# Fetching a weight matrix in pairs of parts with 4 KB rows, and one seam transfer per half

## The chip, the core and the metric

The kernel runs on one core of a Trainium2 chip. Five engines work side by side, each through its own instructions in order: TensorE (PE in the profile; its weight loads are PEld), VectorE (DVE), ScalarE (ACT), GpSimd (POOL) and SyncE (SP), which here only issues DMA transfers. ScalarE and GpSimd issue a few transfers too. The metric is the time of one execution on the device in microseconds; a lower time is better.

## The reference

A gated linear recurrence over complex decays, and then a two-layer network with ELU on its output:

```python
mag = np.sqrt(a_re * a_re + a_im * a_im)
scale = np.minimum(mag, 0.999) / (mag + 1e-06)
a_re_n, a_im_n = (a_re * scale, a_im * scale)
for t in range(S):                       # S = 768, for B = 4, H = 8, D = 48
    ar, ai = (a_re_n[:, :, t, :, None], a_im_n[:, :, t, :, None])
    new_re = ar * S_re - ai * S_im
    new_im = ar * S_im + ai * S_re
    kv = np.einsum('bhd,bhe->bhde', k[:, :, t], v[:, :, t])
    S_re, S_im = (new_re + kv, new_im)
    y[:, :, t] = np.einsum('bhd,bhde->bhe', q[:, :, t], S_re)
x = y.transpose(0, 2, 1, 3).reshape(B * S, H * D)          # 3072 x 384
h = x @ w_in                                               # w_in: 384 x 2048
g = np.where(h > 0.0, h, np.exp(np.minimum(h, 0.0)) - 1.0)
out = g @ w_out                                            # w_out: 2048 x 384
```

The two weight matrices arrive as 64-bit floats, everything else as 32-bit floats.

## The kernel before

**Steps.** The work is cut into twelve steps u = 0 to 11. A step takes 128 positions of two sequences: it loads a (re and im), q, k and v, turns a into running decays (logarithms, sums by matmul, exponentials, sines), scales and rotates q and k by them (`gated`), transposes both on TensorE, multiplies scores and states (`scores`, `states`, `values`), and passes its result through the network (`inner` is the first matmul, `elu` the activation, `project` the second matmul). Steps 0 and 1 and the loading of the weights make up the start; from step 3 on the network's matmuls are done with fewer products, from sums of the weights that are made in between.

**Order.** Every engine works through one order of named pieces. For the start it is written out by hand, in the list `first`; the rest comes from a table of places (`plan`). `warm` pieces are matmuls without a use, put where TensorE would be idle.

**Weights.** `w_in` is held as [128, 3, 2048]: partition p, block i of the contraction, column. Heads are 48 rows wide and a half is 64 partitions, so rows 0 to 47 of a half come from a head of its own and the last 16 from a third of another head. Eight parts of 256 columns are fetched by `fetch("in", m)`, each in four transfers (two of 48 partitions, two of 16), as raw 32-bit words, two to a number, with 2 KB to a row. Their raw words lie in tiles under the tags `g0` and `g1` (parts 0 to 3) and `w64` (parts 4 to 7). `w_out` ([128, 16, 384]) follows in eight parts of its own through `w64`. `rounded` makes a part's 32-bit floats on VectorE with four operations; `convert` steps through them at the places that the list gives: two with one source (L671, L674), a sum of both (L677) and the last that writes `w_in` or `w_out` (L679). These places do not move.

**Seam.** After a step's `values`, its result stands as x (three blocks) and y (the fourth group of heads). `seam` moves the rows of y into the gaps of 16 partitions of x, one small transfer for each half j and block i, six in all. At u = 0 and u = 1 the transfers are spread over SyncE, ScalarE and GpSimd; later they are on GpSimd, with three of one step on SyncE.

## Time and profile before

| | |
|---|---|
| median of 3 runs | 620.69 us (619.47 to 622.34) |
| the profiled execution | 621.27 us, its span 619.5 us |
| TensorE busy | 605.0 us (98%), 6980 matmuls |
| VectorE busy | 503.0 us (81%), 781 operations |
| ScalarE busy | 415.8 us (67%) |
| GpSimd busy | 176.5 us (28%) |
| DMA | 65.54 MB, mean 106 GB/s |
| granted TensorE clock | 0.997 |

The span runs from the first to the last instruction of the profiled execution, and all times inside it count from its start. A row of the timeline gives start, duration, engine, source line, operation, what it writes and reads, and in brackets the idle time of the engine before it with what ended it. A line that begins with `SPq`, `ACTq` or `POOL ... DMA_DIRECT2D` is the issue of a transfer, not the transfer.

### The profile page before, as it was taken

What the parts mean: (1) busy time and instruction counts of PE and PEld (TensorE: products, weight loads), DVE (VectorE), ACT (ScalarE), POOL (GpSimd) and SP (SyncE); (2) the same over time, 40 slices, a digit from 0 to 9 for tenths busy, and PEclk for the clock granted to TensorE, in tenths of its full rate; (3) what the DMA queues carried; (4) which work ended last, traced back from release to release, by engine and by line L of the source; (5) the groups of instructions that cost most, each with busy time, mean ns of one, the idle gap of its engine ahead of it and who ended that gap; (6) DMA issues with size and microseconds to landing.
All of it is one profiled execution on the core that took longest, in us unless ns stands there. A gap on an engine that the chain in (4) does not pass through costs nothing. (4 is left out here: it accounts for less than half of the span.)

```text
span 619.5 us, 16960 instructions
## 1 busy us (share of the span) xinstructions
PE 605.0 (98%) x6980; PEld 550.0 (89%) x6980; DVE 503.0 (81%) x781; ACT 415.8 (67%) x681; POOL 176.5 (28%) x240
## 2 busy tenths in 40 slices
PE   8799999999999999999999999999999999999996
PEld 6678887567899999999999999999999999999996
DVE  5788878667599899888898898899898888984482
ACT  5975674675787667776777876777777777661350
POOL 2000100103113534523524434534534422422000
PEclk9989999999999999999999999999999999999999
DMA  9978739630653253746556545546673647342101
GB/s 165 183 139 136 152 111 239 145 65 22 91 90 58 53 97 81 143 95 123 118 104 123 118 103 121 125 99 122 126 134 85 142 80 132 73 87 66 53 2 32
DMA packets 192179, 65.54 MB, mean 106 GB/s; under 512 B 168116, under 2 KB 181596, under 8 KB 192092
## 3 DMA queue, kind: packets, MB, share of 16 engines
q1 hardware_dynamic: 187920, 62.72, 51.6%
q0 software_dynamic: 3520, 1.20, 1.7%
q8 instruction: 57, 0.93, 0.7%
q10 hardware_dynamic: 652, 0.44, 0.3%
q14 instruction: 30, 0.25, 0.2%
HBM read 48.91 MB, written 4.80 MB: 87 GB/s over the span
## 5 line engine op out<-in xcount | busy, mean ns | idle before, releaser
L1410 PE MATMUL mlp<-w_out,g 128*128 128x192 f32 x640 | 112.1, 328 | 0.0
L1410 PEld LDWEIGHTS mlp<-w_out,g 128*128 128x128 f32 x640 | 104.3, 190 | 3.3 <-DVE ee L1424 0.6
L1132 POOL TENSOR_TENSOR S<-S,T 128x384 f32<-128x384 f32 x36 | 38.0, 1057 | 150.0 <-DVE S L1130 83.1
L1388 DVE TENSOR_TENSOR g<-g 128x512 f32<-128x512 f32 x80 | 60.7, 774 | 6.3 <-PE mlp L1410 4.7
L1301 PE MATMUL mlp<-x,w_in 128*128 128x256 f32 x288 | 64.1, 381 | 0.0
L1301 PEld LDWEIGHTS mlp<-x,w_in 128*128 128x128 f32 x288 | 54.7, 192 | 8.5 <-issue 0.6
L1569 ACT ACTIVATE ee<-g 128x512 f32<-128x512 f32 x63 | 39.6, 629 | 29.5 <-DVE g L1564 26.8
L1548 PE MATMUL mlp<-x,w_in 128*128 128x128 f32 x424 | 56.3, 276 | 0.1
L1410 PE MATMUL mlp<-w,g 128*128 128x192 f32 x320 | 54.5, 329 | 0.0
L1410 PEld LDWEIGHTS mlp<-w,g 128*128 128x128 f32 x320 | 51.8, 190 | 0.6
L1548 PEld LDWEIGHTS mlp<-x,w_in 128*128 128x128 f32 x424 | 51.7, 192 | 0.6 <-DVE g L1564 0.3
L1281 POOL DMA_DIRECT2D x<-y x62 | 30.6, 499 | 72.2 <-ACT y L1177 40.4
L1570 ACT ACTIVATE ee<-ee 128x512 f32<-128x512 f32 x72 | 45.4, 631 | 2.3
L1573 DVE SCALAR_TENSOR_TENSOR g<-ee,g 128x512 f32<-128x512 f32 x63 | 42.4, 682 | 2.3 <-ACT ee L1570 2.3
L1561 ACT COPY g<-mlp 128x512 f32<-128x512 f32 x36 | 20.9, 584 | 29.4 <-PE mlp L1548 29.4
L1564 DVE TENSOR_TENSOR g<-g,mlp 128x512 f32<-128x512 f32 x45 | 30.8, 684 | 8.9 <-PE mlp L1548 4.1
L1291 ACT ACT_TABLE_LOAD x24 | 30.8, 1283 | 2.1 <-issue 1.6
L921 ACT ACTIVATE n<-w 64x384 f32<-64x384 f32 (+1 forms) x60 | 28.1, 486 | 5.2 <-PE w L906 4.4
L1548 PE MATMUL mlp<-x,g 128*128 128x128 f32 x224 | 30.1, 277 | 0.0
L1268 ACT COPY x<-y 128x384 f32<-128x384 f32 x20 | 8.6, 482 | 30.9 <-PE y L1160 30.9
L1075 POOL COPY qt<-kt 32x512 f32<-32x512 f32 x24 | 24.4, 1017 | 16.3 <-PE mlp L1548 10.2
L1548 PE MATMUL y<-x,w_in 128*128 128x128 f32 x216 | 28.5, 275 | 0.0
(218 smaller groups left out, 1369.7 us busy)
## 6 DMA issues: line engine op xcount, KB each, us to landing
w<-in_moe_w_out_dram SPq DMA_DIRECT2D x8, 768.0 KB, 4.7
g<-in_moe_w_in_dram SPq DMA_DIRECT2D x24, 256.0 KB, 3.1
g<-in_moe_w_out_dram SPq DMA_DIRECT2D x24, 256.0 KB, 3.0
w<-in_moe_w_in_dram SPq DMA_DIRECT2D x16, 288.0 KB, 5.8
vn<-in_v_dram SPq DMA_DIRECT2D x24, 192.0 KB, 5.6
qt<-kt SPq DMA_DIRECT2D x72, 64.0 KB, 2.0
kt<-cs SPq DMA_DIRECT2D x72, 64.0 KB, 2.3
q<-in_q_dram SPq DMA_DIRECT2D x11, 384.0 KB, 4.7
```

Source lines behind the costliest of these rows:

```text
L921: nc.scalar.activation(out=flat(x[key][to, n : n + 1]), in_=t[of], func=AF.Exp, scale=sign)
L1132: eng.tensor_tensor(out=new_s, in0=new_s, in1=wide, op=ALU.mult)
L1281: eng.dma_start(out=x["x"][ds(j * HP + D, G), i], in_=x["y"][ds(j * HP + i * G, G)])
L1291: nc.scalar.preload_act_table_set(name)
L1301: nc.tensor.matmul(t[:, e], lhsT=w_in[:, i, ts(f + e, C)], rhs=x["x"][:, i], start=(i == 0), stop=(i == NI - 1),)
L1388: nc.vector.tensor_tensor(out=S_of(u, k, h), in0=a, in1=b, op=op)
L1410: nc.tensor.matmul(to, lhsT=a[:, m], rhs=b[:, m], start=(first and h == 0 and m == 0), stop=False, skip_group_check=True,)
L1548: nc.tensor.matmul(x["c" + c][:, ts(m, C)], lhsT=a[:, m], rhs=x["mix"][p], start=(p == BANKS[c][0] and m == 0), stop=False, skip_group_che ...
L1564: nc.vector.tensor_tensor(out=part(u, to), in0=part(u, a), in1=part(u, b), op=op)
L1569: nc.scalar.activation(out=e, in_=part(u, of), func=AF.Relu, scale=-1.0)
L1570: nc.scalar.activation(out=e, in_=e, func=AF.Exp, scale=-1.0)
L1573: nc.vector.scalar_tensor_tensor(out=part(u, to), in0=nat[u]["e", to], scalar=-1.0, in1=part(u, of), op0=ALU.add, op1=ALU.max,)
```

## The change

**What it does.** w_in is fetched in four pairs of parts, 512 columns at a time, so that a row is 4 KB; the raw words lie in one half or the other of `w_out`, which is not filled yet then. `rounded` still makes one part of 256 columns at a time, from three rows of 256 numbers inside the pair's words. In the list `first`, four `fetch` entries stand where eight stood: the first pair at the place of the first part, the second pair behind the loads of a(1) and v(0) and ahead of q and k of step 1, the third at the place of the old fifth part, and the last at the place of the old seventh. A seam has one transfer for each half (16 x 3 x 256), on SyncE for the first half of steps 0 and 1, on ScalarE for their second half, and on GpSimd after that, but for one half of one step.

```diff
         if kind == "in":
             n = WF * DM // NI
-            dst, cols = w_in[:, :, ts(m, n)], ts(m, 2 * n)
-            tag = "g" + str(m // 2) if m < 4 else "w64"
-            t = sb.tile([C, WF * DM, 2], U32, tag=tag, bufs=2, name="w64")
-            words = t.rearrange("p (i n) two -> p i (n two)", i=NI)
+            dst, cols = None, ts(m, 4 * n)
+            t = w_out[:, ts(m % 2, NF // 2)].rearrange("p f n -> p (f n)").bitcast(U32)
+            words = t.rearrange("p (i n) -> p i n", i=NI)
...
-                last = moe_w_in[ds((2 * NI + j) * D, D), cols].rearrange("(i d) n -> d i n", i=NI)
+                last = moe_w_in[ds((2 * NI + j) * D, D), cols].rearrange("(d i) n -> d i n", i=NI)
...
     def rounded(kind, m):
-        w, dst = raw.pop((kind, m))
-        lo, hi = w[:, :, 0], w[:, :, 1]
         f = sb.tile([C, WF * DM], U32, tag="wt", bufs=2, name="wf")
         r = sb.tile([C, WF * DM], U32, tag="wt", bufs=2, name="wr")
+        if kind == "in":
+            n = WF * DM // NI
+            dst, w = w_in[:, :, ts(m, n)], raw[kind, m // 2][0]
+            w = w.rearrange("p (i n two) -> p i n two", i=NI, two=2)[:, :, ts(m % 2, n)]
+            f, r = (x.rearrange("p (i n) -> p i n", i=NI) for x in (f, r))
+        else:
+            w, dst = raw.pop((kind, m))
+            w = w.rearrange("p (f n) two -> p f n two", f=WF)
+            f, r = (x.rearrange("p (f n) -> p f n", f=WF) for x in (f, r))
+        lo, hi = w[:, :, :, 0], w[:, :, :, 1]
...
     def seam(u):
         x = nat[u]
         for j in range(2):
-            for i in range(NI):
-                eng = nc.scalar if u < 2 and j else nc.gpsimd
-                if u == 0 and i == NI - 1 or u == PAIRED and j:
-                    eng = nc.sync
-                eng.dma_start(
-                    out=x["x"][ds(j * HP + D, G), i], in_=x["y"][ds(j * HP + i * G, G)]
-                )
+            eng = nc.sync if u < 2 and not j or u == PAIRED and j else nc.gpsimd
+            if u < 2 and j:
+                eng = nc.scalar
+            eng.dma_start(out=x["x"][ds(j * HP + D, G)], in_=x["y"][ds(j * HP, D)])
```

In the list `first`, `(fetch, "in", 1)` to `(fetch, "in", 7)` are taken out at their places, and `(fetch, "in", 1)`, `2` and `3`, now pairs, stand in again, for example:

```diff
-        (load_a, 1), (fetch, "in", 1), (load_v, 0), (angles, 0, 0), (fetch, "in", 2),
+        (load_a, 1),  (load_v, 0), (angles, 0, 0), (fetch, "in", 1),
```

**Where the instructions stand.** TensorE's order is the same before and after. Three places of the others follow. First SyncE's transfers at the start, before (`w` with a number is a raw tile of w_in's words, or for `a`, `q` and `k` of step 1 a shared tile; the sizes are those of the first side):

```order
L662 DMA w_146<-in_moe_w_in_dram 48x3x512 x2
L662 DMA w_146<-in_moe_w_in_dram 16x3x512 x2
L611 DMA q<-in_q_dram 128x16x48
L611 DMA k<-in_k_dram 128x16x48
L611 DMA w_193<-in_a_re_dram 128x16x48
L611 DMA w_193<-in_a_im_dram 128x16x48
L662 DMA w_196<-in_moe_w_in_dram 48x3x512 x2
L662 DMA w_196<-in_moe_w_in_dram 16x3x512 x2
L607 DMA vn_72<-in_v_dram 128x8x48 x2
L662 DMA w_205<-in_moe_w_in_dram 48x3x512 x2
L662 DMA w_205<-in_moe_w_in_dram 16x3x512 x2
L611 DMA w_328<-in_q_dram 128x16x48
```

and after:

```order
L661 DMA w_out<-in_moe_w_in_dram 48x3x1024 x2
L661 DMA w_out<-in_moe_w_in_dram 16x3x1024 x2
L611 DMA q<-in_q_dram 128x16x48
L611 DMA k<-in_k_dram 128x16x48
L611 DMA w_192<-in_a_re_dram 128x16x48
L611 DMA w_192<-in_a_im_dram 128x16x48
L607 DMA vn_72<-in_v_dram 128x8x48 x2
L661 DMA w_out<-in_moe_w_in_dram 48x3x1024 x2
L661 DMA w_out<-in_moe_w_in_dram 16x3x1024 x2
L611 DMA w_321<-in_q_dram 128x16x48
```

Twice the bytes of w_in stand ahead of q, k and a, none between a and v, and twice the bytes again ahead of q and k of step 1 (which had two parts ahead of them in two places).

Second, SyncE from the first seam (x<-y) on, before:

```order
L1281 DMA x<-y 16x256 x2
L607 DMA vn_73<-in_v_dram 128x8x48 x2
L662 DMA w_605<-in_moe_w_in_dram 48x3x512 x2
L662 DMA w_605<-in_moe_w_in_dram 16x3x512 x2
L611 DMA ar<-in_a_re_dram 128x16x48
L611 DMA ai<-in_a_im_dram 128x16x48
L662 DMA w_614<-in_moe_w_in_dram 48x3x512 x2
L662 DMA w_614<-in_moe_w_in_dram 16x3x512 x2
L662 DMA w_808<-in_moe_w_in_dram 48x3x512 x2
L662 DMA w_808<-in_moe_w_in_dram 16x3x512 x2
```

and after:

```order
L1286 DMA x<-y 16x3x256
L607 DMA vn_73<-in_v_dram 128x8x48 x2
L661 DMA w_out<-in_moe_w_in_dram 48x3x1024 x2
L661 DMA w_out<-in_moe_w_in_dram 16x3x1024 x2
L611 DMA ar<-in_a_re_dram 128x16x48
L611 DMA ai<-in_a_im_dram 128x16x48
L661 DMA w_out<-in_moe_w_in_dram 48x3x1024 x2
L661 DMA w_out<-in_moe_w_in_dram 16x3x1024 x2
L1286 DMA x<-y 16x3x256
L661 DMA w_914<-in_moe_w_out_dram 128x2x768
```

The second seam's first half has come onto SyncE, behind the last pair and ahead of the first part of w_out.

Third, VectorE around the first conversion (`wr` and `wf` are its two working tiles; L860 is the first step of the angles' turns, n their tile), before:

```order
L671 TENSOR_SCALAR wr<-w_146 128x768
L674 TENSOR_SCALAR wf<-w_146 128x768
L677 ISA wf<-wf,wr 128x1536
L860 SCALAR_TENSOR_TENSOR n<-n,w 128x384
L866 TENSOR_SCALAR cs<-n 128x8x48
```

and after:

```order
L678 TENSOR_SCALAR wr<-w_out 128x768
L681 TENSOR_SCALAR wf<-w_out 128x768
L684 ISA wf<-wf,wr 128x1536
L866 SCALAR_TENSOR_TENSOR n<-n,w 128x384
L872 TENSOR_SCALAR cs<-n 128x8x48
```

Nothing moved here; the operations on a part now read from `w_out`, and their line numbers are six to seven higher.

More of the change, by code (lines that the diff above doesn't have):

```diff
@@ L677, in rounded @@
         yield nc.vector.tensor_tensor(out=f, in0=f, in1=r, op=ALU.add)
-        n = dst.shape[-1]
         nc.vector.scalar_tensor_tensor(
-            out=dst.bitcast(U32), in0=hi.rearrange("p (b n) -> p b n", n=n), scalar=TOP,
-            in1=f.rearrange("p (b n) -> p b n", n=n), op0=ALU.bitwise_and, op1=ALU.bitwise_or,
+            out=dst.bitcast(U32), in0=hi, scalar=TOP, in1=f, op0=ALU.bitwise_and,
+            op1=ALU.bitwise_or,
         )
@@ L1759 @@
         (states, 0, 1), (angles, 1), *2 * [(warm, 2)], (scaled, 1), (noted, 0), (values, 0, 1),
-        (carry_on, 0), (fetch, "in", 3), (convert,), (ends, 1), (convert,), (seam, 0),
-        (load_v, 1), (table, "trig_and_small", 1), (convert,), (warm, 1), (turns, 1), (convert,), (waves, 1), (inner, 0, 2), (inner, 0, 0), (fetch, "in", 4), (load_a, 2), (fetch, "in", 5),
+        (carry_on, 0),  (convert,), (ends, 1), (convert,), (seam, 0),
+        (load_v, 1), (table, "trig_and_small", 1), (convert,), (warm, 1), (turns, 1), (convert,), (waves, 1), (inner, 0, 2), (inner, 0, 0), (fetch, "in", 2), (load_a, 2),
         (table, "natural_log_exp_and_others", 1), (gated, 1, 0), (convert,), (gated, 1, 1),
@@ L1765 @@
         (inner, 0, 4), *2 * [(convert,)], (transposed, 1, "k", 1), (convert,), (warm, 4),
-        (scores, 1, 1), (values, 1, 0), (fetch, "in", 6), (convert,), (fetch, "in", 7),
+        (scores, 1, 1), (values, 1, 0), (fetch, "in", 3), (convert,),
         (states, 1, 1), (convert,), (elu, 0, 0), (convert,), (elu, 0, 4), (values, 1, 1),
```

## The prediction

> **What bounds the kernel now.** I read the busy time by stretch first. Its columns are busy microseconds (with instruction counts) of TensorE, its weight load, VectorE, ScalarE and GpSimd, then the granted clock, the share of the DMA engines and GB/s.
>
> ```profile
> 0.00:42.00 42.00, 35.20 (x409) 29.16 (x410) 30.97 (x46) 33.52 (x62) 5.44 (x33) 1.00 1.03 161
> 42.00:614.00 572.00, 569.64 (x6572) 520.79 (x6572) 471.67 (x735) 382.24 (x620) 171.04 (x207) 1.00 0.51 102
> 42.00:45.00 3.00, 3.00 (x7) 1.79 (x8) 2.09 (x4) 1.85 (x2) 0.00 (x0) 0.50 0.69 130
> ```
>
> From 42 us on TensorE is busy 569.6 of 572 us: an order of matmuls that the change leaves as it is, and that nothing outside TensorE can shorten. So the question is when the matmul row at 42.38 us starts, plus what the half clock in the third row costs just there. Next, the timeline ahead of that point, in order of time: VectorE, then TensorE, then VectorE again.
>
> ```profile
> 16.89 0.56 DVE L860 SCALAR_TENSOR_TENSOR n<-n,w 128x384 f32<-128x384 f32 x1 [3.12 <-ACT n L859]
> 20.00 0.55 DVE L1003 TENSOR_TENSOR k<-k,n 128x384 f32<-128x384 f32 x1
> 24.02 0.96 DVE L1020 TENSOR_TENSOR qg<-q,cs 128x768 f32<-128x768 f32 x1
> 25.25 1.12 PE L1034 MATMUL w<-ident,qg 128*96 128x128 f32 x8
> 26.30 1.15 PE L1082 MATMUL w<-qt,kt 96*64 96x64 f32 x32
> 27.38 1.99 PE L1115 MATMUL mlp<-vn,kg 64*128 64x48 f32 x32
> 29.40 0.56 DVE L1128 TENSOR_TENSOR S<-mlp,T 128x384 f32<-128x384 f32 x1 [1.14 <-PE mlp L1115]
> 38.96 0.95 DVE L999 TENSOR_TENSOR w<-w,n 128x768 f32<-128x768 f32 x1
> 40.70 0.56 DVE L671 TENSOR_SCALAR wr<-w 128x768 uint32<-128x768 uint32 x1
> 41.25 0.18 DVE L968 COPY once<-w 48x32 f32<-48x32 f32 x1
> 41.58 0.38 PE L970 MATMUL w<-once,pair 48*128 48x32 f32 x2 [0.37 <-DVE once L968]
> 42.38 2.77 PE L854 MATMUL w<-n,sum_turns 128*128 128x384 f32 x4
> 44.95 5.59 PE L1301 MATMUL mlp<-x,w_in 128*128 128x256 f32 x24
> ```
>
> The chain is tight. L1020 ends at 24.98 and the transposes that read qg start at 25.25; these end at 26.37, with the scores (L1082) already starting; L1115 follows, and VectorE waited for it before L1128. From there VectorE runs without a gap to L968, which TensorE waits for. The only wide gap is the 3.12 us ahead of L860. A delay that is larger than that gap leaves therefore arrives at 42.38 us nearly whole.
>
> The third view is the DMA side: the stretches (same columns as above), k of the first step as SyncE issues it and the time from its issue to its landing, and VectorE's first conversion.
>
> ```profile
> 2.00:10.00 8.00, 8.00 (x34) 6.89 (x33) 5.30 (x4) 2.67 (x6) 2.33 (x17) 1.00 1.09 193
> 10.00:38.00 28.00, 23.27 (x291) 18.62 (x289) 22.26 (x38) 27.36 (x48) 0.65 (x1) 1.00 1.22 184
> 71.00:73.00 2.00, 2.00 (x11) 1.77 (x10) 1.97 (x4) 1.97 (x4) 0.00 (x0) 1.00 1.08 211
> 76.00:78.00 2.00, 2.00 (x11) 1.77 (x10) 1.85 (x4) 0.94 (x2) 0.00 (x0) 1.00 0.88 356
> 38.00:40.00 2.00, 2.00 (x61) 1.81 (x61) 1.97 (x4) 1.86 (x6) 0.00 (x0) 1.00 0.10 26
> 6.50 4.88 SPq L611 DMA_DIRECT2D k<-in_k_dram  x1
> DMA to landing us min/median/max: 9.3/9.3/9.3
> 11.76 0.56 DVE L671 TENSOR_SCALAR wr<-w 128x768 uint32<-128x768 uint32 x1
> ```
>
> From 2 to 38 us the queue never rests, at 193 and then 184 GB/s: whatever is put ahead delays all that is behind it. k landed at 6.50 + 9.3 = 15.8 us. VectorE converts the first part of w_in at 11.76 with no wait, so that part had landed by then.
>
> **The change, part by part.**
>
> *A longer first fetch.* What stands ahead of q and k grows from one part, 2 x 288 + 2 x 96 = 768 KB, to two: 0.786 MB more, or 4.2 us at the 188 GB/s that I put between the rows of 184 and 211. All four transfers must land before the first conversion. Counted in bytes, a and the part (1.573 MB) are through at 2 + 8.2 = 10.2 us, k (another 0.786) at 14.4; k landed 1.4 later, so the part landed near 11.6, at 11.76 at the latest. With 4.2 us more that is 15.8 to 16.0; I take 16.0, since the last transfers, of 16 partitions, come slowly (the row 38:40, where little else is left).
>
> Whether rows of 4 KB move faster no row says. The two ends are the w_in stretch at 71 us (2 KB rows, transfers of 48 and 16 partitions, 211 GB/s) and the w_out stretch at 76 us (3 KB rows, 128 partitions, 356). I take the w_in end, since the new transfers keep 48 and 16 partitions and the strided source, and differ from it in row length alone. [...]
>
> *Conversion.* The two one-source operations now read three rows of 256 words at a pitch of 1024, where they read one run of 768, and still write one run.
>
> ```profile
> L671 DVE TENSOR_SCALAR wr<-w 128x768 uint32<-128x768 uint32 x12 | 6.7, 558 | 1.1 <-DMA w<-in_moe_w_in_dram 1.1
> L674 DVE TENSOR_SCALAR wf<-w 128x768 uint32<-128x768 uint32 x12 | 6.7, 556 | 0.0
> L679 DVE SCALAR_TENSOR_TENSOR w_in<-w,wf 128x768 uint32<-128x768 uint32 x8 | 7.6, 952 | 0.0
> ```
>
> [...] The bounds are 0.557 (unchanged) and 0.952 each. [...] Price: 0.395 us each, 16 of them, 6.3 us of VectorE, of which only three lie on the chain: two in the first conversion and the one at 40.70. The others fall into VectorE's waits (the 1.14 us ahead of L1128 covers the pair at 26.62) or after 42 us, where VectorE is busy 471.7 of 572 us.
>
> *Sum on the chain.* The first conversion's three operations take from 11.76 to 13.78 now (L677 runs 12.82 to 13.78), 2.02 us; then 2.02 + 0.79 = 2.81. So L860 starts at 16.0 + 2.81 = 18.8 instead of 16.89: +1.9 us, and with 0.2 of it absorbed before 25.25, +1.7. k lands at 15.8 + 4.2 = 20.0 us, ahead of its use at 20.00 + 1.9. With the row at 40.70, +1.7 + 0.4 = +2.1 us.
>
> *a of the second step* comes 4.2 us later as well; ScalarE uses it here:
>
> ```profile
> 22.66 0.84 ACT L736 ACTIVATE n<-w 128x768 f32<-128x768 f32 x1
> 23.41 0.83 ACT L737 ACTIVATE n<-w 128x768 f32<-128x768 f32 x1
> ```
>
> Its two loads end 4.2 us after k's (768 KB more), at about 20.0 now and 24.2 then: L737 waits 0.8 us, less than the 1.7 on the other side, and both sides meet at L1082. They don't add.
>
> *Second pair, q and k of the second step.* Up to this k the queue now moves the bytes that it moved before up to the end of the old fourth part. Most of these had flowed by 38 us (the row 38:40), so k lands at 38 + 1.4 = 39.4 or a little later; L999 needs it at 38.96 + 1.7 = 40.7. Nothing, with a microsecond to spare.
>
> *Third and fourth pair.* Their rows, and those of what follows on SyncE's queue:
>
> ```profile
> 43.47 1.75 SPq L662 DMA_DIRECT2D w<-in_moe_w_in_dram  x4
> 54.99 0.95 DVE L679 SCALAR_TENSOR_TENSOR w_in<-w,wf 128x768 uint32<-128x768 uint32 x1
> 57.58 0.55 DVE L671 TENSOR_SCALAR wr<-w 128x768 uint32<-128x768 uint32 x1
> 65.04 31.35 PE L1301 MATMUL mlp<-x,w_in 128*128 128x256 f32 x144
> 65.48 0.34 ACT L1177 COPY y<-y 128x64 f32<-128x64 f32 x2
> 69.81 0.56 DVE L671 TENSOR_SCALAR wr<-w 128x768 uint32<-128x768 uint32 x1 [0.63 <-DMA w<-in_moe_w_in_dram]
> 71.69 0.83 ACT L736 ACTIVATE n<-ar 128x768 f32<-128x768 f32 x1
> ```
>
> The third pair's issue follows the one at 43.47; with v of step 1 ahead (0.393 MB, 2.1 us) and 8.4 us of its own it is through at 54.0 and lands by 55.4, ahead of 57.58. a of step 2, behind it, comes 4.2 us later and is used at 71.69. The raw words lie in halves of w_out, so the fourth pair waits on SyncE until the fourth part is converted, at 56; behind it are queued seam(1)'s first half, which came from GpSimd's queue, and the w_out fetches. Moved behind a from 58 to 66.4, it serves the conversion at 69.81, which today waits 0.63 for its data: a wait goes, off the path. seam(1) can't be issued before y at 65.82 anyhow; its data follow at 66.4, and the hidden layer of step 1 reads them two groups of 12 into the 144, at 65.04 + 2 x 2.61 = 70.3. Covered by some 2 us; without that cover TensorE would wait.
>
> *Seams.* Six transfers become two.
>
> ```profile
> 40.44 1.23 SPq L1281 DMA_DIRECT2D x<-y  x2
> 40.45 1.50 ACTq L1281 DMA_DIRECT2D x<-y  x2
> 40.72 1.10 POOL L1281 DMA_DIRECT2D x<-y  x2 [21.47 <-ACT y L1177]
> ```
>
> Issue at u = 0 shortens by about half, but x is read at 44.95, after L854 has ended: nothing. Later it relieves GpSimd, busy 171 of 572 us: nothing either.
>
> Together +2.1 us on the profiled execution, 621.27 (span 619.50 and 1.77 around it), gives 623.4. The median of the runs is 620.69, 0.58 lower; the forecast for the median is **622.8 us**. A measurement here tells from no change about 0.5%, 3.1 us, so this counts as the same.
>
> **Rivals.**
>
> *Row length decides* (not slower). If 4 KB rows go at the 356 GB/s of w_out, the pair lands at about 12.0, the conversion ends at 14.8, and the gap ahead of L860 swallows all of it. The point of decision is a landing by 16.89 - 2.81 = 14.1 us, which 1.573 MB reach at 240 GB/s. Only the 0.4 us at 40.70 is left: 621.1. Against it: the transfers' shape. For it: 356 beside 211.
>
> *The tail doubles* (slower by over 0.5%). In the row 38:40 only 26 GB/s flow: the old fourth part trails off for 2 us. A pair of twice the size may trail twice as long before its last transfer lands: two more microseconds ahead of the first conversion, +4.1, 624.8. It decides from a landing of 17.0 us on. For it: SyncE's transfers of 16 partitions come last; against it: part of that trail was there at 11.76 already, and is in the 16.0.
>
> *VectorE keeps its speed* on three rows: L860 at 18.0, +1.1 - 0.2, and nothing at 40.70; then ScalarE's 0.8 counts alike. +0.9: 621.6.
>
> *The half clock goes away.* L854's four matmuls took 2.77 us at clock 0.50, where the same four took 1.45 earlier:
>
> ```profile
> 14.78 1.45 PE L854 MATMUL w<-n,sum_turns 128*128 128x384 f32 x4
> ```
>
> If the shift moves L854 out of that stretch, 1.3 to 1.5 us come back: 621.4 with the rest as forecast. It can also fall on other work, and goes with any case.
>
> **How the numbers follow.** Forecast 0.50, row length 0.20, tail 0.14, VectorE's speed kept 0.10, something else (seam(1) late, among others) 0.06. Range 619.5 to 625.4: below, row length with the clock's 1.5 off; above, the tail and half a microsecond of spread (the runs before lie 1.2 and 1.7 us around their median). The likeliest alone: 621.4 to 624.0. Faster than 617.6 would need more than all of the above to go well: 0.03. Slower than 623.8: a quarter of the forecast's 0.50, most of the tail's 0.14, a part of the rest: 0.27. Same: 0.70.
>
> **What the profile after would show.** First conversion: a wait of 3 to 5 us on a DMA ahead of it, start near 16.0; 14 or less means row length. Its two one-source rows near 950 ns (right) or 557 (wrong). L737's counterpart waiting some 0.8 us for a. TensorE's turns near 44.5 us, with the 570 us behind it as before. GB/s between 4 and 14 us near 190. Wrong altogether, if TensorE shows new waits after 45 us, above all at step 1's hidden layer, or if the conversion starts after 17 us.

## The result, and the profile after

| | before | after |
|---|---|---|
| median of 4 runs beside each other | 621.52 us (619.47 to 624.0) | 637.83 us (634.6 to 639.18) |
| the profiled execution, its span | 621.27, 619.5 us | 634.6, 632.9 us |
| TensorE busy, VectorE busy, GpSimd busy | 605.0, 503.0, 176.5 us | 609.8, 509.0, 157.6 us |
| granted TensorE clock | 0.997 | 0.983 |

The changed kernel takes 1.0273 times as long (95% interval 1.0242 to 1.0304): 16 us more, where the forecast was 2. The profiled execution is the shortest of its four, so it shows 13.4 us of the loss; what the other three lose beyond it was not profiled. All times here and below come from fast executions; of run 15's two, 635.12 us at a granted clock of 0.983 and 644.85 at 0.977, that leaves the first.

The timeline of the kernel after at the same places as before (up to the turns, line numbers are six or seven higher: L860 is now L866, and the turns' matmuls L854 are now L860). VectorE's first conversion, then TensorE, then ScalarE's second half of a, then both engines up to the turns:

```profile
17.30 0.95 DVE L678 TENSOR_SCALAR wr<-w_out 128x768 uint32<-128x768 uint32 x1 [5.61 <-DMA w_out<-in_moe_w_in_dram]
18.17 0.94 DVE L681 TENSOR_SCALAR wf<-w_out 128x768 uint32<-128x768 uint32 x1
...
20.02 0.55 DVE L866 SCALAR_TENSOR_TENSOR n<-n,w 128x384 f32<-128x384 f32 x1
...
22.05 0.60 PE L976 MATMUL w<-once,pair 48*128 48x32 f32 x2 [3.49 <-DVE once L974]
...
25.24 0.84 ACT L743 ACTIVATE n<-w 128x768 f32<-128x768 f32 x1 [0.50 <-DMA w<-in_a_im_dram]
...
42.37 0.96 DVE L1005 TENSOR_TENSOR w<-w,n 128x768 f32<-128x768 f32 x1 [0.19 <-DMA w<-in_k_dram]
...
44.12 0.94 DVE L678 TENSOR_SCALAR wr<-w_out 128x768 uint32<-128x768 uint32 x1
...
45.30 0.60 PE L976 MATMUL w<-once,pair 48*128 48x32 f32 x2 [0.95 <-DVE once L974]
...
46.42 2.58 PE L860 MATMUL w<-n,sum_turns 128*128 128x384 f32 x4
```

The first conversion starts at 17.30 us after 5.61 us of waiting, L866 at 20.02 instead of 16.89, and the turns at 46.42 instead of 42.38: 4.04 us late. Of these, 3.13 are there at L866; 0.28 more come up to L1005 (0.19 of them its wait for k), 0.3 from the conversion at 44.12, and 0.3 since the two matmuls at 45.30 and those behind them run at half clock (granted 0.50 from 45.30 to 48.00 us). Here is what comes behind, TensorE's states(1,1), its y, and the first matmuls of step 1's hidden layer, which stood at 65.04 us before:

```profile
65.84 1.14 PE L1121 MATMUL w<-vn,kg 64*64 64x48 f32 x63
74.62 0.23 PE L1121 MATMUL w<-vn,kg 64*64 64x48 f32 x1 [7.64 <-issue]
74.74 1.24 PE L1157 MATMUL y<-a,vn 64*64 64x64 f32 x32
...
76.94 2.50 PE L1304 MATMUL mlp<-x,w_in 128*128 128x256 f32 x5
```

"[7.64 <-issue]" says that TensorE stood still ahead of the last of 64 matmuls and waited for nothing that the profile shows. The kernel before has a small wait of the same kind at the same matmul:

```profile
63.59 0.26 PE L1115 MATMUL w<-vn,kg 64*64 64x48 f32 x2 [0.26 <-issue]
```

The hidden layer starts 11.9 us late: 4.04 at the turns, and 7.86 between them and here. The rest is in the stretches (the columns are those of the prediction; the seventh, behind the five engines, is the granted clock):

```profile
21.40:28.20 6.80, 6.14 (x28) 5.97 (x29) 5.98 (x13) 5.42 (x9) 0.65 (x1) 0.50 1.06 178
69.20:79.40 10.20, 4.78 (x55) 3.98 (x55) 4.48 (x7) 0.87 (x4) 0.00 (x0) 0.50 0.42 59
80.00:627.00 547.00, 544.81 (x6192) 499.50 (x6191) 451.54 (x701) 367.74 (x590) 152.70 (x165) 1.00 0.49 98
```

A stretch at half clock (0.50, from 69.2 us) begins within the stall and goes on behind it; from 80 us on the kernel runs as before. So 4.04 + 7.86 = 11.9. Of the last 1.5 us of 13.4, some 1.2 are the hidden layer's first 2.46 us (76.94 to 79.40), which run at a granted clock of 0.50; 0.3 isn't placed. The first stretch at half clock cost little: VectorE, on whose results TensorE waits there, was 3.13 us late at L866 and 3.27 at the first product behind it (L1026, 23.74 instead of 20.47).

Two more views say what TensorE waited for. The first is the queues of the DMA engines, in two stretches of the kernel after, and then in two of the kernel before: packets, megabytes, and their share of the 16 engines' time. q1 is SyncE's queue; q8 carries instructions (57 packets and 0.93 MB on the page, so 16 KB each; TensorE's 6980 matmuls and 6980 weight loads would be 245 to a packet, an estimate that counts nothing else in them).

```profile
q1 hardware_dynamic: 1584, 1.56, 106.8%
```

This is 61 to 71 us after, and it is the only queue in that stretch: 1.56 MB of data, and no instructions for 10 us. From 71 to 73 us:

```profile
q1 hardware_dynamic: 73, 0.21, 85.3%
q8 instruction: 1, 0.02, 5.5%
```

The first block of instructions comes when the data run out: its packet runs from 71.30 to 73.05, and TensorE goes on at 74.62, 1.57 us later. Before, from 58 to 61 us (data) and 61 to 62 us (instructions):

```profile
q1 hardware_dynamic: 6, 0.01, 1.7%
```

```profile
q8 instruction: 1, 0.02, 5.6%
```

There the queue was all but empty (0.01 MB in 3 us), since SyncE was holding the next part of w_in back for a free `w64` tile (its issues go on at 62.7 us), and data flowed again only from 63 us on. The block's packet ran from 61.14 to 62.04, and the matmul behind the small wait started 1.55 us later. In every wait of this kind over 0.25 us in the first 100 us, in all runs below, the matmul behind it starts 1.2 to 1.9 us after the end of such a packet, which ties the wait to the fetch.

Where the queue is idle (before, and in runs 2, 7 and 10), this packet begins within 0.8 us of TensorE's 602nd matmul, 127 ahead of the place where the block is needed; here it begins 7.3 us behind it (64.01 and 71.30 us). The 127 matmuls between are short: TensorE is through them in 2.75 us. The last view is SyncE after, around the fourth pair:

```profile
49.26 9.57 SPq L611 DMA_DIRECT2D ai<-in_a_im_dram  x1
59.62 3.74 SPq L661 DMA_DIRECT2D w_out<-in_moe_w_in_dram  x4
77.63 0.58 SPq L1286 DMA_DIRECT2D x<-y  x1
```

The whole fourth pair, 1.57 MB, is queued from 59.6 to 63.4 us, just ahead of the 602nd matmul. The seam's transfer behind it leaves at 77.63, when its data exist; TensorE doesn't wait for it.

### The profile page after: what moved, and what is told of

It reads as the page before. It is cut to its first block, busy times and chain, and to the rows that moved or that the text cites. A ratio compares the mean times of both kernels' runs of the same rounds, so it can differ in the third digit from the quotient of the medians.

```text
span 632.9 us, 16805 instructions
## 1 busy us (share of the span) xinstructions
PE 609.8 (96%) x6980; PEld 554.7 (88%) x6980; DVE 509.0 (80%) x781; ACT 416.7 (66%) x681; POOL 157.6 (25%) x197
## 4 chain that ended last, share of the span: by engine, by line
PE 85%; SPq 5%; DMA 4%; issue 2%; ACT 1%; DVE 1%; POOL 0%; DVEq 0%; POOLq 0%; ACTq 0%
PE mlp L1413 28%; PE mlp L1551 15%; PE mlp L1304 10%; PE y L1551 8%; PE w L1121 4%; PE y L1166 3%; PE y L1329 3%; PE mlp L1329 3%; PE y L1236 3%; SPq L611 2%; DMA w<-in_k_dram 2%; PE w L860 2%; PE y L1157 2%; PE w L1040 2%; PE w L912 1%
## 5 line engine op out<-in xcount | busy, mean ns | idle before, releaser
L1138 POOL TENSOR_TENSOR S<-S,T 128x384 f32<-128x384 f32 x36 | 39.7, 1103 | 148.4 <-DVE S L1136 82.6
L1121 PE MATMUL w<-vn,kg 64*64 64x48 f32 x1280 | 25.8, 220 | 8.1 <-issue 8.1
L1136 DVE TENSOR_TENSOR S<-w,S 128x384 f32<-128x384 f32 x38 | 20.9, 551 | 14.1 <-PE w L1121 12.7
```

Source lines behind the costliest of these rows:

```text
L1121: nc.tensor.matmul(to, lhsT=of, rhs=vn[u % 2][ts(c, L), n, ts(h, D)], start=True, stop=True,)
L1138: eng.tensor_tensor(out=new_s, in0=new_s, in1=wide, op=ALU.mult)
```

## The experiments

Theory after the result: the loss is a late start (the pair in front) and TensorE's instructions held up behind the fourth pair, each with a stretch at a granted clock of 0.50. Rivals: the stall is a semaphore or the place in the program; the new conversions, w_out as the place of the raw words, or the seams cost something. Unless a sentence says otherwise, ratios are to the kernel before, run beside each.

**1. The seam alone, in the kernel before.** `seam` as in the change, fetches as before. Here w_in's rows for the third group of heads keep their old order, so the 16-partition gaps meet other rows of w_in; the work is the same.

```diff
-            for i in range(NI):
-                eng = nc.scalar if u < 2 and j else nc.gpsimd
...
+            eng = nc.sync if u < 2 and not j or u == PAIRED and j else nc.gpsimd
+            if u < 2 and j:
+                eng = nc.scalar
+            eng.dma_start(out=x["x"][ds(j * HP + D, G)], in_=x["y"][ds(j * HP, D)])
```

> The kernel before with the new seam alone: one transfer per half, the first half of steps 0 and 1 from SyncE. My theory puts the whole 16 us on the fetches and nothing on the seams: 621 us, within 0.3% of the kernel before, and no wait of TensorE over 0.5 us near 64 us. The rival, that the second seam on SyncE's queue disturbs the start of step 1's hidden layer or GpSimd's later work, would show here as at least 2 us more.

Measured: 629.47 us, 1.013 (1.0091 to 1.0169). The theory missed. SyncE's queue, and TensorE's wait:

```profile
51.37 19.85 SPq L662 DMA_DIRECT2D w<-in_moe_w_in_dram  x12
71.32 0.59 SPq L1280 DMA_DIRECT2D x<-y  x1
...
76.55 28.92 PE L1298 MATMUL mlp<-x,w_in 128*128 128x256 f32 x120 [5.58 <-DMA x<-y]
```

In the order of before, SyncE holds the last parts of w_in back until a `w64` tile is free, and the seam behind them leaves at 71.32 us. TensorE waits 5.58 us, and from 75.4 to 82.1 us the granted clock is 0.50. In the kernel after nothing waits ahead of it.

**2. The last pair behind the second seam.** In the kernel after, in `first`:

```diff
-        (scores, 1, 1), (values, 1, 0), (fetch, "in", 3), (convert,),
+        (scores, 1, 1), (values, 1, 0), (convert,),
...
-        (seam, 1), *2 * [(convert,)],
+        (seam, 1), (fetch, "in", 3), *2 * [(convert,)],
```

> The kernel after with one entry moved: the last pair is issued behind the second seam instead of ahead of states(1,1), so that the DMA queues are idle when TensorE needs its next 16 KB of instructions near 65 us. Theory (the fetch of TensorE's instructions is held up behind the fourth pair's data): TensorE's 7.6 us of waiting for nothing that the profile shows goes, and the half clock behind it too, 8 to 9.5 us in all: 628 to 630 us. First rival (the stall belongs to a semaphore of the converted weights or to states(1,1) itself): it stays, 637 us. Second rival (the fetch is held up by whatever is moved, a(2) and the third pair included): the stall stays in part, 2 to 4 us, 632 to 634 us. The conversion of the seventh part comes later in each case; TensorE needs that part only some 30 us later, so it costs nothing.

Measured: 638.69 us, 1.0304 (1.0274 to 1.0335). The time says rival, the trace says theory:

```profile
68.07 1.15 PE L1121 MATMUL w<-vn,kg 64*64 64x48 f32 x64
...
85.95 0.95 DVE L678 TENSOR_SCALAR wr<-w_out 128x768 uint32<-128x768 uint32 x1 [10.11 <-DMA w_out<-in_moe_w_in_dram]
...
87.55 4.92 PE L1304 MATMUL mlp<-x,w_in 128*128 128x256 f32 x11 [9.06 <-DVE g L1315]
```

All 64 matmuls run through and the 7.64 us are gone. But VectorE waits 10.11 us for the late pair, with step 0's ELU (g) behind that conversion in its order, and TensorE waits 9.06 us for g. The expectation had counted only when TensorE needs that part of w_in, not what stands behind its conversion.

**3. Rows of 2 KB at the same places.** Each pair in eight transfers instead of four:

```diff
-            dst, cols = None, ts(m, 4 * n)
+            dst = None
...
+            for h in range(2):
+                cols, to = ts(2 * m + h, 2 * n), words[:, :, ts(h, 2 * n)]
```

> The kernel after with each pair fetched as two parts with 2 KB to a row, eight transfers where four stood, at the same places and into the same raw words; nothing else is changed. If the number of bytes in the queue holds up TensorE's instructions, the stall near 67 us stays at 6 to 8 us and the time at 636 to 638 us. If the length of one row does (the instruction fetch waits for a turn of rows twice as long), the stall falls to 3 to 4 us and the time to about 633 us. The start: if 4 KB rows made the first pair trail off, the first conversion starts at 16 us here instead of 17.3; with the bytes alone it starts at 17 again or, since the first part's own transfers are through earlier, near 17 as long as the conversion waits for the whole pair, and near 13 if it waits only for its part.

Measured: 629.18 us, 1.0133 (1.0091 to 1.0174), 8.7 us less than the kernel after. Neither side of the expectation had that: the stall lies between theirs, the time below both. The first conversion, and the stall:

```profile
16.66 0.95 DVE L680 TENSOR_SCALAR wr<-w_out 128x768 uint32<-128x768 uint32 x1 [5.45 <-DMA w_out<-in_moe_w_in_dram]
...
70.38 0.23 PE L1123 MATMUL w<-vn,kg 64*64 64x48 f32 x1 [4.41 <-issue]
```

And how fast the fourth pair flows, with nothing beside it, first after (64 to 72 us, 4 KB rows), then here (61 to 67 us); the last column is GB/s:

```profile
64.00:72.00 8.00, 2.98 (x135) 2.65 (x132) 2.14 (x4) 3.12 (x8) 0.00 (x0) 0.82 1.05 142
```

```profile
61.00:67.00 6.00, 4.98 (x158) 4.52 (x157) 4.10 (x6) 3.40 (x9) 0.00 (x0) 1.00 1.08 182
```

Here rows of 4 KB flow at 142 GB/s, rows of 2 KB at 182. The pair drains sooner, TensorE's block comes sooner (its packet ends at 68.83), and the stall is 4.41 us.

**4 and 5. More data in the kernel before.** A pair that nobody reads is added behind the sixth part (`extra`, into w_out's first half), in run 4 with 4 KB rows, in run 5 with 2 KB rows.

```diff
-        (fetch, "in", 4), (load_a, 2), (fetch, "in", 5),
+        (fetch, "in", 4), (load_a, 2), (fetch, "in", 5), (extra,),
```

> The kernel before with one pair of 4 KB rows (1.57 MB, words that nobody reads) added to SyncE's queue behind the sixth part, so that data are moved between 55 and 66 us, where its queue was empty. Theory (data in the queue hold up TensorE's instruction fetch): a wait of TensorE that shows no releaser comes up at 63.6 us in states(1,1), where before had 0.26 us, now 3 to 8 us, and the time goes to 625 to 631 us with the half clock behind it. Rival (the stall comes from the new conversion or from w_out as the place of the raw words, not from the queue): no such wait, 621 to 622.5 us, the seventh part coming some us later at most.

Measured: 625.36 us, 1.0089 (1.0056 to 1.0122).

```profile
63.33 0.34 PE L1127 MATMUL w<-vn,kg 64*64 64x48 f32 x2 [2.75 <-issue]
```

With the old conversions, the old place of the raw words and the old seams, the stall comes up as soon as the queue is full at that time: 2.75 us, just below the 3 to 8 expected. (TensorE also waits 1.64 us for g at 77.30, as in run 2, since the seventh part comes later.)

> The kernel before with the same 1.57 MB added at the same place as in the run before this one, but with 2 KB to a row and eight transfers. If it is bytes in the queue that hold up TensorE's instructions, its wait in states(1,1) is there again, somewhat shorter than the 2.75 us with 4 KB rows because rows of 2 KB flow faster (some 180 GB/s against 140, by the runs so far): 1 to 2.75 us, 623 to 625 us. If only rows of 4 KB hold them up, there is no wait beyond the 0.26 us of the kernel before, and the time is 620 to 621.5 us.

Measured: 628.33 us, 1.0152 (1.0122 to 1.0182).

```profile
57.65 7.74 SPq L674 DMA_DIRECT2D w_out<-in_moe_w_in_dram  x2
...
61.10 0.26 PE L1129 MATMUL w<-vn,kg 64*64 64x48 f32 x2 [0.31 <-issue]
...
76.16 26.04 PE L1315 MATMUL mlp<-x,w_in 128*128 128x256 f32 x108 [5.57 <-DVE g L1326]
```

This run doesn't answer its question: SyncE held the second half of the added words back (7.74 us), from 58 to 65 us only 78 GB/s flowed, and the stall is 0.31 us. The second half of the added words was not in the queue when the block was wanted. Its 5.57 us are the loss of run 2: the seventh part comes late, and g stands behind its conversion.

**6 and 7. Parts at the old places.** Run 6 fetches parts 0 to 3 by themselves, at the places of before, into their columns of the shared half of w_out; run 7 does so with all eight, parts 6 and 7 behind the second seam.

```diff
+            half = kind == "part"
+            g = m // 2 if half else m
+            t = w_out[:, ts(g % 2, NF // 2)].rearrange("p f n -> p (f n)").bitcast(U32)
...
+            if half:
+                cols, words = ts(m, 2 * n), words[:, :, ts(m % 2, 2 * n)]
...
-        (load_a, 1),  (load_v, 0), (angles, 0, 0), (fetch, "in", 1),
+        (load_a, 1), (fetch, "part", 1), (load_v, 0), (angles, 0, 0), (fetch, "part", 2),
```

> The kernel after with its first two pairs fetched as four parts with 2 KB to a row at the places of the kernel before; the third and the fourth pair stay as they are, 4 KB to a row. Theory (the start and the stall are two separate costs): TensorE's turns come back to about 42.4 us, 4 us earlier, and the wait near 67 us stays at 7 to 8 us, now near 63: 633.5 to 634.5 us at the median. Rival (the wait ends when the queue has drained, and the queue isn't earlier by as much): TensorE comes to the place 4 us earlier and waits 2 to 4 us longer, 636 to 638 us. Second rival (without the late start the data flow out of step with the instruction fetch): the wait goes, 625 us.

> The kernel after with the raw words still in w_out, the conversions still from three rows and one seam transfer for each half, but all eight parts fetched by themselves with 2 KB to a row: parts 0 to 5 at the places of the kernel before, parts 6 and 7 behind the second seam, so that nothing flows while TensorE fetches its instructions near 61 us. Theory (the whole loss comes from where and when the data of w_in flow): no wait of TensorE over 0.6 us behind 45 us, 620 to 622 us, equal to the kernel before. Rival (the place in w_out, the slower conversions or the seam cost something too): 623 us or more. VectorE will wait 1 to 3 us for part 6 near 70 us; that should reach TensorE with nothing.

Measured: 637.68 us, 1.0273 (1.022 to 1.0325), and 637.65 us, 1.0312 (1.0269 to 1.0355). Neither is near its theory; run 6's stall in states(1,1) was there as expected, 7.65 us, but at 79.79 us. VectorE's last operation on part 0 in run 6 and TensorE behind it; then TensorE near 83 us in run 7:

```profile
26.21 0.96 DVE L689 SCALAR_TENSOR_TENSOR w_in<-w_out,wf 128x768 uint32<-128x768 uint32 x1 [3.41 <-DMA w_out<-in_moe_w_in_dram]
...
28.19 1.91 PE L1044 MATMUL w<-ident,qg 128*96 128x128 f32 x8 [3.21 <-DVE qg L1030]
```

```profile
82.87 25.08 PE L1308 MATMUL mlp<-x,w_in 128*128 128x256 f32 x108 [6.64 <-DVE g L1319]
```

Part 0 had long landed. The operation waits for part 1 (2.75 us in run 7), whose columns lie between part 0's in the same half of w_out and whose fetch comes ahead in the order; run 11, with a place for each part, has no such wait. In run 6 TensorE then stood for 3.21 us, and from 27.5 to 41.1 us the granted clock was 0.50, with TensorE busy 12.91 of 13.6 us. In run 7 there is no stall in states(1,1), as expected, but parts 6 and 7 came late for VectorE, as in run 2.

**8. Rows apart.** In the kernel after, wf (f) has gaps between its rows.

```diff
-        f = sb.tile([C, WF * DM], U32, tag="wt", bufs=2, name="wf")
+        f = sb.tile([C, NI, 264], U32, tag="wt", bufs=2, name="wf")
...
+            f, r = f[:, :, 0:n], r.rearrange("p (i n) -> p i n", i=NI)
```

> The kernel after with the working tile of the second one-source operation laid out as three rows of 256 words with a gap of 8 words behind each, so that this operation writes three rows as it reads three; the first one-source operation still writes one run of 768. Theory (double speed needs the rows of source and output to match): the second one-source operation falls from 0.94 to 0.56 us, the first stays at 0.95; 0.39 us less at the first conversion, 637.4 us, which can't be told from the kernel after. Rival (the strided source alone costs the speed): both stay at 0.95 us.

Measured: 636.11 us, 1.0264 (1.0232 to 1.0297), which can't be told from the kernel after. The second one-source operation of the first conversion:

```profile
19.41 0.68 DVE L682 TENSOR_SCALAR wf<-w_out 128x768 uint32<-128x768 uint32 x1
```

With matching rows it takes 0.68 us, while the first, unchanged, takes 0.95: most of the speed comes back, but three short rows are not one run (0.56). Neither side had that number.

**9. The seam alone, without SyncE at step 1.** As run 1, but w_in's rows have the order that goes with the new seam, and another engine issues the first half at step 1. Against run 1:

```diff
-            eng = nc.sync if u < 2 and not j or u == PAIRED and j else nc.gpsimd
+            eng = nc.sync if u < 1 and not j or u == PAIRED and j else nc.gpsimd
```

> The kernel before with one seam transfer for each half, and the last heads' rows of w_in in the order that goes with it; at step 1 the first half's transfer is issued by GpSimd, not by SyncE. Theory (in the run with the seam alone, the 5.6 us of TensorE came from the transfer standing on SyncE's queue behind a fetch that waits for its buffer): no wait on x<-y, 619.5 to 621 us, the kernel before. Rival (one transfer of 48 KB over 16 partitions is itself slow or late): a wait of some us on x<-y stays, 624 us or more.

Measured: 620.36 us, 1.0001 (0.9981 to 1.0021). One transfer for each half costs nothing and gains nothing; in run 1 the place in SyncE's queue cost the time.

**10. The last pair late, and its conversions too.** As run 2, with four `convert` entries moved from ahead of `(inner, 1, 4)` to places behind `(load_a, 3)`.

```diff
-        (inner, 0, 8), (inner, 0, 6), (convert,), (elu, 0, 8),
-        (convert,), (inner, 1, 6), (inner, 1, 0), (fetch, "out", 0), (convert,), (inner, 1, 2), (elu, 0, 6), (convert,),
+        (inner, 0, 8), (inner, 0, 6), (elu, 0, 8),
+        (inner, 1, 6), (inner, 1, 0), (fetch, "out", 0), (inner, 1, 2), (elu, 0, 6),
```

> The kernel after with the last pair behind the second seam, as in the run with the last pair late, and with the four conversion steps of the seventh part put some 12 us later in VectorE's order, behind the activations that TensorE waits for. Theory (in that run the 9 us of TensorE were VectorE's wait for the pair, with the ELU of step 0 queued behind it): neither the 7.6 us in states(1,1) nor the 9.1 us on g is there, and no half clock follows; only the late start of 4 to 5 us is left of the loss: 624.5 to 626.5 us. Rival (late data cost TensorE something wherever they are put): a wait of 3 us or more stays somewhere between 60 and 100 us, 629 us or more.

Measured: 635.72 us, 1.0244 (1.0211 to 1.0277). The expectation was 10 us too low. VectorE's wait for the pair, then TensorE:

```profile
87.74 0.95 DVE L678 TENSOR_SCALAR wr<-w_out 128x768 uint32<-128x768 uint32 x1 [5.71 <-DMA w_out<-in_moe_w_in_dram]
...
92.64 3.75 PE L1304 MATMUL mlp<-x,w_in 128*128 128x256 f32 x8 [4.87 <-DVE w_in L685]
```

Both old waits are gone, but the pair needs 13.8 us from its issue at 73.92 to the conversion, and TensorE waits 4.87 us for w_in itself. The rival was right: at each place that was tried, this pair either covers the instruction fetch or comes late.

**11. A quarter of w_out for each part.** All of the change but its pairs:

```diff
-            dst, cols = None, ts(m, 4 * n)
-            t = w_out[:, ts(m % 2, NF // 2)].rearrange("p f n -> p (f n)").bitcast(U32)
+            dst, cols = w_in[:, :, ts(m, n)], ts(m, 2 * n)
+            t = w_out[:, ts(m % 4, NF // 4)].rearrange("p f n -> p (f n)").bitcast(U32)
```

Parts 0 to 5 are fetched at the places of before, parts 6 and 7 behind the second seam, with run 10's order of conversions.

> All that the change brings besides its pairs: raw words in w_out, one seam transfer for each half, the same engines for the seams. Each part has 2 KB rows, a quarter of w_out of its own, so that a conversion reads one run of 768 and waits for its own part alone; parts 0 to 5 are fetched at the places of the kernel before, parts 6 and 7 behind the second seam, with the conversion steps late as in the run before. Theory (the loss lies in the order and the length of w_in's transfers, and in what waits for them): TensorE's turns at 42.4 us, no wait over 0.6 us after them, 619 to 621 us. If the 0.5 us in states(1,1) of the kernel before was held up by the fetch of part 4 and 5 too, it stays. Rival (raw words in w_out or the seams cost something): 623 us or more.

Measured, over 12 runs: 619.61 us, 0.9991 (0.9972 to 1.001). It equals the kernel before; that it is better isn't shown. The turns, the states and the only larger wait behind them:

```profile
41.20 1.46 PE L859 MATMUL w<-n,sum_turns 128*128 128x384 f32 x4
...
59.50 1.15 PE L1120 MATMUL w<-vn,kg 64*64 64x48 f32 x64
...
78.13 15.78 PE L1303 MATMUL mlp<-x,w_in 128*128 128x256 f32 x72 [0.44 <-DVE w_in L684]
```

The turns take 1.46 us for four here, where before took 2.77 at a granted clock of 0.50, and states(1,1) has no wait at all.

**12. The first pair split.** Part 0 at the start and part 1 behind a of step 1, each in its quarter; the other three pairs are the change's.

```diff
-        (warm, 1), (warm, 12), (fetch, "in", 0),
+        (warm, 1), (warm, 12), (fetch, "part", 0),
...
-        (load_a, 1),  (load_v, 0),
+        (load_a, 1), (fetch, "part", 1), (load_v, 0),
```

> The kernel after with only the first pair split: part 0 at the start with 2 KB to a row, part 1 behind a of step 1, each in a quarter of w_out of its own; the other pairs are unchanged. Theory (the start and the stall in states(1,1) are separate): the first conversion starts near 12 us, TensorE doesn't wait 3.5 us at 22 us, the half clock at 21 to 28 us is gone, and its turns start at 42.4 to 43.5 us; the stall stays at 7 to 8 us with half clock behind it: 632 to 634 us. Rival (the stall takes up what the start gains, since the queue drains at the same time): the stall grows to 10 us or more, 636 us.

Measured: 636.0 us, 1.0257 (1.0224 to 1.029).

```profile
40.79 0.39 PE L1163 MATMUL y<-a,vn 64*64 64x64 f32 x10 [2.78 <-issue]
...
46.49 2.77 PE L866 MATMUL w<-n,sum_turns 128*128 128x384 f32 x4
...
75.62 0.24 PE L1127 MATMUL w<-vn,kg 64*64 64x48 f32 x1 [8.26 <-issue]
```

The first conversion is back at 12.17 us, and still the turns start at 46.49: a second wait of the issue kind, 2.78 us at 40.79, ate the gain. The second pair flows just ahead of it. The rival had the time and not the mechanism: the stall in states(1,1) is 8.26 us, not 10, and the gain went at the earlier block. The two losses aren't separate, as the theory had it: the second pair, too, can hold up a block that TensorE comes to sooner.

**13 to 16.** Runs 13, 15 and 16 have more or fewer warm matmuls at the very start (`(warm, 12)` becomes 28, 4 and 20), so that all that follows has another number in TensorE's count of matmuls. If a block of instructions that has not arrived makes the stall (the theory), the stall keeps its number, the 729th, and leaves its place in the program; the rival keeps the place. Run 14 keeps rows of 4 KB and cuts each pair into twelve transfers, one for each block i.

```diff
-                pairs.append((words[ds(j * HP, D)], heads[j]))
+                for i in range(NI):
+                    pairs.append((words[ds(j * HP, D), i], heads[j][:, i]))
```

> The kernel after with 28 warm matmuls where the list's second entry has 12, so that all of TensorE's later instructions lie 16 matmuls (32 instructions) further on. [...] Rival (the stall belongs to this place in the program: a semaphore, a buffer, the last matmul of the group): it stays ahead of the last matmul of states(1,1), number 745 by count. The extra matmuls run while TensorE waits for its first data, and cost nothing: 636 to 639 us in both cases.

Measured: 635.47 us (630.59 to 639.09), 1.0244 (1.018 to 1.0309). The profiled execution, the shortest of four, has no large wait at either place (TensorE waits 2.83 us for ScalarE at 77.27 instead), so it decides nothing on the 7.64 us. Of a small one it does: ahead of the 349th or 350th matmul by count, which was in y (L1163, run 12) and now is in the states:

```profile
41.32 0.31 PE L1121 MATMUL mlp<-vn,kg 64*128 64x48 f32 x1 [0.38 <-issue]
```

> The kernel after with each pair fetched in twelve transfers instead of four, one for each block of the contraction, 48 or 16 partitions by one row of 4 KB. If rows of 4 KB are what flows slowly, the first conversion starts at 17 to 18.5 us as in the kernel after, the stall in states(1,1) stays at 7 to 8.5 us, and the time at 636 to 639 us. If the size or the number of the transfers is what counted in the run with 2 KB rows (it had eight), this one has the conversion near 16.6 us, a stall of 4 to 5 us and 628 to 630 us.

Measured: 631.5 us, 1.0172 (1.0135 to 1.0209).

```profile
17.74 0.95 DVE L680 TENSOR_SCALAR wr<-w_out 128x768 uint32<-128x768 uint32 x1 [6.46 <-DMA w_out<-in_moe_w_in_dram]
...
58.60 15.22 SPq L663 DMA_DIRECT2D w_out<-in_moe_w_in_dram  x12
...
67.34 0.20 PE L1123 MATMUL w<-vn,kg 64*64 64x48 f32 x1 [1.90 <-issue]
```

Each side is right in part. The conversion is as late as with four transfers of 4 KB rows (17.74), so the number of transfers is not what makes it late. But the stall is 1.90 us, less than either side had: SyncE gives out the twelve over 15 us instead of four in 3.7, so less can stand in the queue when TensorE's block is wanted. The fourth pair flowed at 164 GB/s here (63 to 69 us), between the 142 and the 182 of run 3, so row length alone doesn't set that rate.

> The kernel after with 4 warm matmuls where the list's second entry has 12: TensorE's later instructions all lie 8 matmuls nearer to the start. Theory (a 16 KB block of instructions has not arrived): the stall stays ahead of the 729th matmul by count, which is now 8 matmuls later in the program: states(1,1) runs through its 64 matmuls, and the wait of several us falls into the y matmuls behind it (32 of one row), after 7 to 9 of them. Rival (it belongs to the place): the wait stays ahead of the last of the 64, number 721 by count. 634 to 639 us in both cases.

> The kernel after with 20 warm matmuls where it has 12: TensorE's later instructions all lie 8 matmuls further on. Theory: the wait of several us comes 8 matmuls earlier in the program, after 54 to 56 of the 64 of states(1,1). Rival: it stays ahead of the last of them, number 737 by count. 634 to 639 us in both cases, if the longer warm stretch doesn't delay the start beyond the first pair's landing; and the stall may be small or missing, as with 16 more, if the fetch falls between transfers.

Measured: 635.12 us in run 15 (one execution) and 635.74 in run 16 (two). TensorE in run 15, then in run 16:

```profile
66.19 0.42 PE L1157 MATMUL y<-a,vn 64*64 64x64 f32 x14
74.91 0.80 PE L1157 MATMUL y<-a,vn 64*64 64x64 f32 x18 [8.29 <-issue]
```

```profile
66.51 0.91 PE L1121 MATMUL w<-vn,kg 64*64 64x48 f32 x47
74.60 0.68 PE L1121 MATMUL w<-vn,kg 64*64 64x48 f32 x17 [7.18 <-issue]
```

The stall left its place: with eight warm matmuls fewer it comes 15 matmuls later, after 14 of the y matmuls; with eight more it comes 16 earlier, after 47 of the 64. By count it stays behind TensorE's 728th or 729th. (The shift is twice what was expected, since a warm matmul shows as two in the trace: the kernel after has 26 of L1646 at the start for 13 in the list.) A semaphore, a buffer or the last matmul of a group would have moved with the program. The waits of this kind in the first 100 us of all runs lie behind matmuls 348, 602 and 729, or one fewer or more: 254 and 127 apart. 127 matmuls with a weight load each are 254 instructions, near the 245 to a packet estimated above, so the spacing fits one block. A late fetch need not cost TensorE anything. In the kernel before, the block needed at the 602nd matmul was fetched late too, through a full queue (182 GB/s from 53.6 to 57.3 us; its packet began at 57.32, 3.7 us behind the 475th matmul), but those 127 matmuls take 6.8 us, and TensorE didn't wait; the next 127 take 2.75.

## Why the prediction was wrong

**The step that failed** is the one on the third and fourth pair. It priced them at nothing: "it serves the conversion at 69.81, which today waits 0.63 for its data: a wait goes, off the path." It asked who reads the pair's data and what is queued on SyncE, and not what else the DMA engines carry: TensorE's instructions. 7.9 us and some 1.2 us of half clock, of 13.4, come from there. The row for it stood in the timeline of before, [0.26 <-issue] in states(1,1), with the queue idle around it; it was not used. The sentence that nothing outside TensorE can shorten its 570 us was true, and no ground for taking that nothing lengthens them. The list of signs named new waits after 45 us and a conversion after 17; both came, though the place was states(1,1), not the hidden layer.

**The first pair's landing** was mis-sized: 16.0 forecast, 17.30 measured, and 18.0 to 18.7 in the six other profiles that begin with the same transfers (runs 2, 8, 10, 13, 15, 16). In the kernel after, the rate was not at fault, as this stretch shows (the last column is GB/s):

```profile
4.00:14.00 10.00, 8.93 (x37) 6.75 (x37) 6.47 (x6) 6.06 (x11) 0.57 (x6) 1.00 1.04 184
```

The forecast had "near 190". The end was: by the trace's DMA records nine tenths of the pair's rows had begun by 13.77 us, and the last tenth took 2.2 us more, where the old first part's took 1.2 (9.68 to 10.89 us), run 3's with 2 KB rows 1.1, and run 14's, at 182 GB/s up to 14 us, 2.6. So "the tail doubles" came nearest, in its landing past 17.0 and in its mechanism; that its +4.1 nearly met the 4.04 at the turns is luck, since its landing was 18.0 and 0.9 us came on behind L866. In runs 2, 8 and 10 the queue also moved less from 4 to 14 us (170, 160 and 164 GB/s); why, isn't shown. "Row length decides" had the wrong sign: each of the four pairs took longer from its first row to its last with 4 KB rows (10.0 to 12.5 us) than in run 3 (9.1 to 10.1). At 142 GB/s the fourth pair's 1.57 MB take 11 us, where 8.4 was forecast.

**The conversion** was right: 0.95 and 0.94 us for the one-source operations, and VectorE busy 6.0 us longer, forecast 6.3. That three rows of 256 would take the upper bound, the 0.952 us of the operation with two sources, was the author's estimate; why they take 0.95 isn't shown, and where the output has three rows too, in run 8, it is 0.68. At the conversion ahead of the turns it cost 0.3 us (0.86 from 44.12 to the next operation, 0.55 before), forecast 0.4. L866 at 20.02 instead of 18.8 is the landing again.

**a of the second step** was right (0.50 us of waiting, forecast 0.8, not on the path). **q and k of the second step**: nothing forecast, 0.19 us measured, but by luck: k landed near 42.37, where 39.4 was forecast, and that stayed hidden because VectorE was itself late. **The seams** were right for this order, and run 1 shows that it hung on the order: behind a fetch that waits for a tile, the same transfer costs 9 us.

**The half clock** went the other way than its rival: where before had one stretch of 3 us, after has 0.50 from 21.4 to 28.2 and from 69.2 to 79.4 as well, each beginning within a wait of TensorE over 3 us (3.49 and 7.64).

The chance for slower, 0.27, was low mainly because every rival ended in the start.

## What to carry to other kernels

Before moving large transfers, look at the instruction packets on the DMA queues and at TensorE's waits "issue": a gap between transfers can be what lets the next block of instructions through (the one of 58 to 63 us before), and filling it can stop an engine that waits for no data (7.64 us after, 2.75 in run 4), above all where its instructions are short and a block of them is soon used up (127 matmuls in 2.75 us). Ask of a late transfer not only who reads it but what is queued behind its first reader, on the reading engine and on the issuing queue. And take a row's rate from rows of the same length: the fourth pair moved at 142 GB/s with rows of 4 KB and at 182 with rows of 2 KB.

## What was not expected of the hardware

- Instructions can wait for data: 10 us without one packet of q8 while 1.56 MB went through q1, and stalls of 7.2 to 8.3 us in six profiled kernels (after, runs 6, 8, 12, 15, 16) with a pair of 4 KB rows queued just then. Runs 13 and 14 got the block through in the middle of the pair. In the six, SyncE had issued the whole pair when TensorE came to its 602nd matmul, or had by 0.3 us later; in runs 13 and 14 it was still issuing it for 3 and 11 us. That fits a fetch that stands behind what was queued before it, but no run moved only this, and the cause is open.
- Rows of 4 KB into 48 and 16 partitions, the fourth pair: 142 GB/s in four transfers and 164 in twelve, with 182 for 2 KB rows. Why, isn't shown; the first pair doesn't show it up to 14 us (184 and 183).
- A one-source operation over three rows of 256: 0.95 us into one run of 768, 0.68 into three rows, 0.56 from run to run.
- A wait of about 3 us can cost TensorE more behind it: 3.21 us in run 6 were followed by 13.6 us at half clock, though TensorE was busy for 12.91 of them.
